# Gates by tanh, a last block in batch pairs, more turns on the matrix engine and a new order in a gated recurrence with a feed-forward

## The chip, the cores and the metric

One core of a Trainium2 chip runs the kernel. The metric is the time of one execution on the device in microseconds, the median over the runs shown.

## What is computed

An attention of the mLSTM kind over 4 batches, 8 heads, 768 steps and head size 40, and behind it a gated feed-forward of width 320 (the heads side by side). Cut to what matters:

```
m_new = max(f_t + m, i_t);  f' = exp(f_t + m - m_new);  i' = exp(i_t - m_new)
C = f' C + i' v_t k_t^T;    n = f' n + i' k_t
y_t = sigmoid(o_t) * (C q_t) / max(|n q_t|, 1)

x = y of all heads side by side                       # (4, 768, 320)
gate = sigmoid(causal convolution of x over 5 steps, one filter per column)
out = (gate * (x @ w_val)) @ w_out
```

The feed-forward's three weights come as float64, everything else as float32.

## The kernel before

The 768 steps are cut into six blocks j of 128 and each block into two halves of 64. A unit u = (j, b) is one block of one batch; a step g of 48 is one half of a unit. For each step, `args` computes the exponents of the decay by one matmul and `expo` their exponential; `scores` multiplies keys by queries; `probs` masks and scales on DVE; `keyw` weighs the keys on POOL; `heads` applies them to the values and, in the same run of matmuls, makes the next state, which `state_out` copies on ACT behind the values, where the next step reads it. So the steps of one batch form a chain.

Ahead of that, queries and keys are prepared per block, batch and side (x = 0 queries, x = 1 keys): `prep_max` finds the largest value on ACT, `prep_hi` and `prep_lo` split the scaled numbers in two-byte parts, stacked in one of three tiles `stk`, and the stack is turned, either by a DMA transpose from SP's queue (`prep_tr`, line 402) or on PE by eight transposes and a copy on ACT (`turn_pe`, line 410, and `turn_out`). The function `TURN` picks the way: before, all of block 0 and the queries of block 1 go over PE, 12 turns.

Behind the heads, `norm_abs`, `norm_rec`, `norm_o` and `gate_o` divide and apply the output gate, `x_tr` transposes the unit's result and `x_copy` puts it into `xc` (two chunks of 128 columns) and `x3` (64 columns; batches 0 and 1 in the lower partitions, 2 and 3 in the upper). From these, `feed(j)` makes the feed-forward of a block: `conv` (one instruction on ACT and four on DVE per chunk), `sigmoid`, `val` (x @ w_val on PE), `z_mul` on DVE, `outp` on PE, a copy and a store. In the last block it runs in two parts, batches 0 and 1, then 2 and 3.

The gates i and f are scanned in log form on DVE at the start, spread through DRAM and gathered as matmul operands; the weights are converted from float64 by integer steps on DVE, POOL and ACT.

The order of all 1141 operations is written out by hand: `PLAN` gives each operation of each kind its place in one sequence, and each engine and each DMA queue works through its share of it strictly in that order. `BANKS` gives each matmul group one of eight PSUM banks. DMAs are issued from SP's queue, apart from the spreading of the gates, which ACT issues.

Of the kernel before, what the change touches and what calls it, by code (L numbers as in the profile page):

```python
# [16 lines left out]
NTK, NSTK, NDM, NPT, NKW, NOB, OJ = 4, 3, 4, 3, 3, 3, 3  # L17
PLAN = {
# [31 lines left out]
    "args": (  # L50
        "223 220 236 237 274 281 266 285 311 322 334 351 354 369 387 397 414 488 474 472 581 550 582 585 638 640 "
        "666 675 688 738 712 741 763 816 772 814 835 893 873 910 916 974 901 976 1029 1025 1035 1055"
    ),
    "expo": (
        "229 247 244 240 277 288 272 293 316 327 340 361 358 378 392 403 417 502 515 491 591 578 596 614 641 647 "
        "670 679 695 744 716 749 767 821 777 818 838 897 877 915 926 980 907 982 1036 1027 1039 1059"
    ),
    "scores": (
        "241 226 246 258 284 289 291 307 324 332 359 356 396 384 401 419 485 495 501 531 584 587 594 634 642 677 "
        "681 686 708 760 753 758 807 817 812 831 880 909 878 914 972 992 945 994 1033 1046 1048 1062"  # L60
    ),
    "probs": (
        "245 254 249 264 295 298 303 310 337 341 363 373 400 440 413 426 490 506 520 535 597 592 601 637 649 685 "
        "690 693 715 769 756 764 813 830 822 837 884 911 890 920 981 997 962 1017 1040 1049 1054 1065"
    ),
    "keyw": (
        "242 257 253 261 282 294 309 314 331 339 345 371 383 424 411 428 492 513 524 538 598 593 602 622 650 655 "
        "674 691 704 751 734 752 783 825 790 833 846 905 892 921 952 956 1041 1042"
    ),
    "heads": (  # L70
        "250 267 260 275 300 317 326 338 344 362 375 391 406 451 422 439 526 537 543 557 615 628 621 645 668 696 "
        "702 728 732 775 765 782 828 840 845 869 904 918 896 938 988 1009 998 1030 1050 1064 1060 1066"
    ),
    "state": (
        "263 280 270 283 312 323 333 352 355 438 386 399 415 465 436 482 533 546 554 564 624 636 630 654 684 703 "
        "710 733 739 803 774 800 832 871 859 874 913 928 902 946 999 1004 1056 1063"
    ),
    "nabs": (
        "278 287 335 346 370 427 489 497 567 563 643 653 705 735 784 793 863 881 959 957 1023 1034 1067 1069"
    ),  # L80
    "nrec": "290 347 437 500 568 656 736 794 882 960 1037 1070",
    "rs": (
        "299 304 357 365 446 442 504 509 573 571 660 662 747 746 802 799 885 888 963 965 1044 1043 1073 1075"
    ),
    "x": (
        "308 360 367 377 460 448 512 514 579 575 663 671 773 748 847 849 891 917 977 979 1057 1045 1079 1080"
    ),
    "x_tr": (
        "313 372 388 382 468 463 522 534 595 589 755 683 810 836 875 912 968 970 983 985 1068 1058 1083 1086"
    ),  # L90
    "xc": (
        "348 380 394 389 484 470 528 539 605 600 761 687 815 841 887 919 971 975 989 991 1072 1061 1091 1095"
    ),
    "w_d": "71 64 61 23 67 97 234 243 302 423",
    "w_v": (
        "88 113 140 142 149 170 154 186 192 204 224 227 233 235 238 239 259 268 271 279 315 321 379 393 407 416 "
        "434 445 464 473 467 471 477 479 494 503"
    ),
# [6 lines left out]
    ),  # L105
    "conv0": "450 447 519 612 609 603 805 780 770 930 936 922 995 1001 1018 1074 1081 1076 1097 1109 1107",
    "conv": (
# [4 lines left out]
    ),  # L112
# [7 lines left out]
    ),  # L120
    "od": (
        "620 743 707 709 762 850 848 844 898 903 944 942 987 990 1015 1013 1052 1053 1088 1092 1132 1135 1138 "
        "1140"
    ),
}
BANKS = {
    "turn": "035214670217",
    "args": "456253054116722220154136320117150322715637044021",
    "scores": "432504700614456444555014006335324055110067647044",
    "ph": "623501366516421627255123",  # L130
    "pc": "44375644173345241133224470663034305631416020700",
    "x_tr": "766401332772034403237672",
    "conv": "724753757036037640552",
    "val": "270507314471263371406",
    "outp": "403206323674017663512173",
}
ENG = {}


def TURN(j, x, i):  # L140
    return 1 if j == 0 or (x == 0 and j == 1) else 0
# [3 lines left out]
def tile_mlstm_gated_ffn(  # L145
# [78 lines left out]
    tk_ = ring(NTK, [P, L + H * (P + L)], F16, "tk")  # L224
# [9 lines left out]
    rs_ = ring(2, [P, H, D], F32, "rs")  # L234
# [16 lines left out]
    def fill_v(kind, default, out, v):  # L251
        eng(kind, default).memset(out, v)

# [142 lines left out]
    def turned(j, x, i):  # L396
        if x == 0:
            return tq_[j % 2][:, i]
        return tk_[(j * B + i) % NTK][:, L:].rearrange("k (h n) -> k h n", h=H)[:, :, 0:P]
# [51 lines left out]

    def heads(g):
        u, p = divmod(g, 2)
        j, b = divmod(u, B)
        if p == 0:
            ph[u] = bank("ph", u, H, DT)
        more = g < NG - 2 * B or p == 0
# [417 lines left out]
```

## Time and profile before

| | us |
|---|---|
| median of 3 runs | 237.76 |
| lowest, highest | 235.78, 238.15 |
| span of the profiled execution | 234.1 |

| engine | busy us | share of the span |
|---|---|---|
| PE (matmuls) | 183.8 | 78% |
| DVE | 188.3 | 80% |
| ACT | 172.8 | 74% |
| POOL | 109.0 | 47% |

The span runs from the first to the last instruction of one profiled execution; the runs are timed without a profile and include what lies around it. PE is the matrix engine, PEld its weight loads, DVE the vector engine, ACT the scalar engine, POOL GpSimd, SP the queue that issues most DMAs. A float32 matmul appears as two records. Busy shares are means over stages with different limits.

### The profile page before, as it was taken

The page shows a single profiled execution, that of the slowest core. Times are in us where ns is not written, and L with a number is a line of the kernel's source. Part 1 is how long each engine was busy: PE and PEld are TensorE (multiplying, and loading weights), DVE is VectorE, ACT ScalarE, POOL GpSimd, SP SyncE. Part 2 cuts the span into 40 slices and gives each one's busy share as a digit, 9 for nine tenths or more (in the row PEclk, how much of TensorE's full clock was granted, in tenths as well). Part 3 has the DMA queues.
Part 4 walks back from the last instruction along what each step waited for, and adds up shares of the span by engine and source line. Part 5 has one row for each costly group of instructions (what it writes and reads, how often), then busy time and mean ns, then how long its engine had stood idle before and what let it go on. Part 6 is the DMA issues. An engine that isn't in the chain of part 4 may idle for free.

```text
span 234.1 us, 6369 instructions
## 1 busy us (share of the span) xinstructions
PE 183.8 (78%) x2432; PEld 135.4 (58%) x2432; DVE 188.3 (80%) x409; ACT 172.8 (74%) x357; POOL 109.0 (47%) x165
## 2 busy tenths in 40 slices
PE   0016501888997578699899999998999999999993
PEld 0016401666886545476768776875876776785441
DVE  7969988998798799999998869958798295539920
ACT  4584993999999996989969889598965846344431
POOL 7656404387789637835378375534632000420000
PEclk9999999999998577999999999999999999999999
DMA  6999997999999999999989999999167110001011
GB/s 112 174 174 178 195 162 100 148 181 182 140 156 176 204 174 209 152 181 147 201 190 196 164 183 175 160 213 184 62 79 159 59 56 0 30 31 59 0 55 59
DMA packets 146599, 31.96 MB, mean 137 GB/s; under 512 B 142408, under 2 KB 145864, under 8 KB 146568
## 3 DMA queue, kind: packets, MB, share of 16 engines
q1 hardware_dynamic: 144936, 31.25, 87.8%
q10 hardware_dynamic: 1632, 0.30, 0.7%
q8 instruction: 19, 0.31, 0.6%
q14 instruction: 12, 0.10, 0.1%
HBM read 17.87 MB, written 4.23 MB: 94 GB/s over the span
## 4 chain that ended last, share of the span: by engine, by line
PE 42%; ACT 18%; DVE 16%; SPq 8%; DMA 7%; issue 6%; ACTq 1%; POOL 0%; POOLq 0%; DVEq 0%
PE pb L463 12%; PE pb L610 9%; DVE pb L545 7%; PE pb L581 5%; SPq L336 4%; PE pb L612 3%; PE pb L421 3%; PE pb L434 3%; ACT junk L353 3%; DMA sg<-in_o_gate_dram 3%; DMA nat<-in_q_dram 3%; ACT sg L558 2%; ACT stk L381 2%; PE pb L503 2%; SPq L844 2%
## 5 line engine op out<-in xcount | busy, mean ns | idle before, releaser
L463 PE MATMUL pb<-vc,pt 128*64 128x41 f32 (+1 forms) x768 | 54.8, 235 | 6.3 <-ACT vc L249 4.0
L463 PEld LDWEIGHTS pb<-vc,pt 128*64 128x64 f32 (+1 forms) x768 | 50.0, 143 | 13.9 <-ACT vc L249 6.2
L446 POOL TENSOR_TENSOR kw<-kp,dm 128x320 f32<-128x320 f32 (+1 forms) x44 | 33.5, 771 | 38.4 <-ACT dm L424 26.7
L465 PE MATMUL pb<-vc,kw 128*40 128x41 f32 (+1 forms) x704 | 44.1, 218 | 0.4 <-ACT dm L424 0.2
L439 DVE SCALAR_TENSOR_TENSOR pt<-pb,cmp,dm 128x512 f32<-128x512 f32 x48 | 34.4, 737 | 11.0 <-PE pb L434 8.6
L465 PEld LDWEIGHTS pb<-vc,kw 128*40 128x40 f32 (+1 forms) x704 | 39.6, 119 | 0.8 <-issue 0.3
L410 PE MATMUL pb<-ident,stk 128*120 128x128 f16 x96 | 12.4, 318 | 33.0 <-DVE stk L387 33.0
L387 DVE SCALAR_TENSOR_TENSOR stk<-nat,scl,stk 128x320 f16<-128x320 f32 x48 | 32.9, 705 | 4.9 <-POOL stk L383 2.5
L383 POOL TENSOR_SCALAR stk<-nat,scl 128x640 f16<-128x640 f32 x24 | 21.5, 903 | 23.4 <-DMA vc<-in_v_dram 11.4
L410 PEld LDWEIGHTS <-stk 128*120 128x120 f16 x96 | 10.8, 219 | 34.2 <-DVE stk L387 34.2
L491 POOL TENSOR_TENSOR rs<-sg,den 128x320 f32<-128x320 f32 x24 | 18.0, 769 | 26.2 <-DVE den L487 25.4
L545 DVE SCALAR_TENSOR_TENSOR pb<-xc,cwt,pb 128x512 f32<-128x512 f32 (+1 forms) x42 | 27.4, 672 | 2.9 <-ACT pb L541 2.4
L610 PE MATMUL pb<-wall,zt 128*128 128x320 f32 x96 | 29.1, 442 | 0.4 <-DVE zt L602 0.4
L424 ACT ACTIVATE dm<-pb 128x512 f32<-128x512 f32 x48 | 27.3, 596 | 2.3 <-PE pb L421 1.7
L353 ACT ACTIVATE junk<-nat 128x320 bf16<-128x320 f32 x48 | 22.5, 469 | 6.6 <-DMA nat<-in_q_dram 5.8
L381 ACT ACTIVATE stk<-nat,scl 128x640 f16<-128x640 f32 x24 | 19.0, 819 | 9.6 <-DVE scl L359 4.8
L434 PEld LDWEIGHTS <-tk 120*128 120x128 f16 x384 | 15.8, 99 | 11.7 <-issue 9.1
L249 ACT COPY vc<-pb 40x328 f32<-40x328 f32 x44 | 18.8, 433 | 4.9 <-PE pb L465 3.1
L434 PE MATMUL pb<-tq,tk 120*128 120x64 f16 x384 | 18.4, 195 | 4.7 <-ACT vc L249 2.6
L610 PEld LDWEIGHTS pb<-wall,zt 128*128 128x128 f32 x96 | 17.3, 189 | 8.1 <-issue 1.3
L249 POOL COPY kp<-nat 64x640 f32<-64x640 f32 x24 | 18.6, 778 | 3.3 <-DMA nat<-in_k_dram 2.1
L249 ACT COPY ob<-pb 128x320 f32<-128x320 f32 x24 | 9.4, 428 | 14.4 <-PE pb L612 13.9
(108 smaller groups left out, 348.1 us busy)
## 6 DMA issues: line engine op xcount, KB each, us to landing
vc<-in_v_dram SPq DMA_DIRECT2D x12, 320.0 KB
sg<-in_o_gate_dram SPq DMA_DIRECT2D x6, 640.0 KB
out_dram<-ob SPq DMA_DIRECT2D x24, 160.0 KB
nat<-in_k_dram SPq DMA_DIRECT2D x10, 320.0 KB
nat<-in_q_dram SPq DMA_DIRECT2D x10, 320.0 KB
nat<-in_k_dram SPq DMA_DIRECT2D x4, 160.0 KB
nat<-in_q_dram SPq DMA_DIRECT2D x4, 160.0 KB
raw<-in_moe_w_val_dram SPq DMA_DIRECT2D x2, 320.0 KB
```

The source lines that it names most:

```text
L249: (e.copy if e is nc.scalar else e.tensor_copy)(out, in_)
L353: nc.scalar.activation(junk, part(j, x, i), AF.Abs, accum_out=amx[j % 2][:, x, i : i + 1])
L381: nc.scalar.activation(o, v, AF.Copy, scale=f)
L387: nc.vector.scalar_tensor_tensor(t[:, :, lo : lo + D], part(j, x, i), scl[j % 2][:, x, i : i + 1], t[:, :, 0:D], op0=ALU.mult, op1=ALU.sub ...
L424: nc.scalar.activation(dm_[g % NDM], psd[g], AF.Exp)
L434: nc.tensor.matmul(pss[g][:, h], tk[h], tq[:, h], start=True, stop=True)
L439: nc.vector.scalar_tensor_tensor(pt_[g % NPT], pss[g], cmp_[j % 2][:, p, b : b + 1], dm_[g % NDM], op0=ALU.mult, op1=ALU.mult)
L446: eng("keyw", "P").tensor_mul(kw_[g % NKW][0:n], kp[0:n, p, b * H : (b + 1) * H], dm_[g % NDM][0:n, :, L - 1 : L].to_broadcast([n, H, D]),)
L463: nc.tensor.matmul(ph[u][p * L : (p + 1) * L, h], pt_[g % NPT][0:n, h], mv, start=True, stop=True)
L465: nc.tensor.matmul(pc[g][n0 : n0 + D, h], kw_[g % NKW][0:n, h], mv, start=True, stop=True)
L545: nc.vector.scalar_tensor_tensor(of(gt, c, b0, b1) if t == 4 else o, x, w, o, op0=ALU.mult, op1=ALU.add)
L610: nc.tensor.matmul(t, zz[0][:, c, b], wo[:, c], start=(c == 0), stop=False)
```

## The change

Both gates are computed by tanh: sigmoid(a) = (1 + tanh(a/2)) / 2. The additions of 1 go into the products that follow (`gate_o`, `z_mul`, now of three operands), the factors into the function's scale (0.25 for the convolution, whose input is twice as large, 0.5 for the output gate) and into the scale of the last copy (0.25). The output gate is computed by an instruction of its own per block (`tanh_o`), the convolution's gate by another (`gate_x`). The division moves: DVE multiplies heads and output gate first (`gate_o`), and POOL multiplies by the reciprocal behind it (`norm_x`).

In the last block the batches are taken in the order 0, 2, 1, 3, and its feed-forward runs in the pairs (0, 2) and (1, 3), which lie in different partition halves of `x3`; the gate is applied per chunk.

Turns on PE take all 128 columns of the stack in place of 120, and there are 23 of them: all 8 of block 0, and in each later block the queries of batch 0 and the keys of batches 0 and 2. 25 DMA transposes remain of 36. `PLAN` and `BANKS` are written anew for all 1155 operations.

```diff
+TURNS = (((0, 1, 2, 3), (0, 1, 2, 3)),) + (((0,), (0, 2)),) * 5
 def TURN(j, x, i):
-    return 1 if j == 0 or (x == 0 and j == 1) else 0
+    return i in TURNS[j][x]
...
+    def jb(u):
+        j, b = divmod(u, B)
+        return j, (0, 2, 1, 3)[b] if j == NJ - 1 else b
+
+    def both(q):
+        return slice(q, B, B2)
...
-            nc.tensor.transpose(t[0:K3, h], stack(j, x, i)[:, h, 0:K3], ident16)
+            nc.tensor.transpose(t[:, h], stack(j, x, i)[:, h], ident16)
...
-    def norm_o(u):
-        j, b = divmod(u, B)
-        eng("rs", "P").tensor_mul(
-            rs_[u % 2], og[j % 2][:, b * H : (b + 1) * H], den[u // 2 % 3][:, u % 2, :, None].to_broadcast([P, H, D])
-        )
-
     def gate_o(u):
-        nc.vector.tensor_mul(x_[u % 2], ph[u][:, :, 0:D], rs_[u % 2])
+        j, b = jb(u)
+        o = og[j % 2][:, b * H : (b + 1) * H]
+        nc.vector.scalar_tensor_tensor(y_[u % 2], o, 1.0, ph[u][:, :, 0:D], op0=ALU.add, op1=ALU.mult)
+
+    def norm_x(u):
+        d = den[u // 2 % 3][:, u % 2, :, None].to_broadcast([P, H, D])
+        eng("x", "P").tensor_mul(x_[u % 2], y_[u % 2], d)
...
-    def sigmoid(j, b0, b1):
-        if b1 - b0 < B:
-            for g in (gt[0][:, :, b0:b1], of(gt, 2, b0, b1)):
-                nc.scalar.activation(g, g, AF.Sigmoid)
-            return
-        jo = j + OJ
-        g = sg[:, ng[0] : ng[1]]
-        if jo < NJ:
-            g = sg[:, 0 : ng[1]] if jo % 2 == 0 else sg[:, ng[0] :]
-        nc.scalar.activation(g, g, AF.Sigmoid)
-
-    def sig_o(j):
-        nc.scalar.activation(og[j % 2], og[j % 2], AF.Sigmoid)
+    def gate_x(j, c, qs):
+        g = sg[:, ng[0] : ng[1]] if c is None else of(gt, c, qs)
+        nc.scalar.activation(g, g, AF.Tanh, scale=0.25)
+
+    def tanh_o(j):
+        nc.scalar.activation(og[j % 2], og[j % 2], AF.Tanh, scale=0.5)
...
-            nc.vector.tensor_mul(of(zz, m, b0, b1), s, of(gt, m, b0, b1))
+        nc.vector.scalar_tensor_tensor(o, t, 1.0, s, op0=ALU.add, op1=ALU.mult)
...
-        copy("ob", "A", ob_[(j * B + b) % NOB], pot[j, b])
+        nc.scalar.activation(obs(j, b), pot[j, b], AF.Copy, scale=0.25)
...
     def feed(j):
-        n = B if j < NJ - 1 else B2
-        for b in range(0, B, n):
-            feed_part(j, b, b + n)
+        for qs in [(0, 1)] if j < NJ - 1 else [(0,), (1,)]:
+            feed_part(j, qs)
```

## Rows read from the trace of the kernel before

**Rows 1.** Stages: window, us, PE, PEld, DVE, ACT, POOL busy, clock, DMA share, GB/s.
```profile
0.00:44.10 44.10, 11.07 (x88) 9.86 (x89) 38.89 (x104) 29.72 (x57) 23.30 (x47) 1.00 1.05 153
44.10:75.00 30.90, 27.28 (x585) 21.74 (x584) 26.68 (x54) 29.77 (x69) 23.76 (x30) 1.00 1.25 173
75.00:95.00 20.00, 14.04 (x183) 10.49 (x182) 18.27 (x42) 17.89 (x42) 12.11 (x18) 0.66 1.17 189
95.00:120.00 25.00, 22.66 (x327) 16.78 (x327) 24.05 (x49) 21.56 (x49) 12.99 (x20) 1.00 1.36 173
120.00:208.00 88.00, 86.58 (x1173) 64.85 (x1171) 66.08 (x130) 63.85 (x121) 35.39 (x51) 1.00 0.73 122
208.00:234.10 26.10, 22.12 (x84) 11.66 (x81) 14.32 (x35) 10.01 (x23) 1.41 (x2) 1.00 0.11 39
```

**Rows 2.** ACT's table loads by line: count, busy us, mean ns, idle before.
```profile
L424 ACT ACT_TABLE_LOAD x7 | 9.0, 1283 | 0.1
...
L558 ACT ACT_TABLE_LOAD x5 | 6.4, 1283 | 2.1 <-DMA sg<-in_o_gate_dram 2.0
...
L561 ACT ACT_TABLE_LOAD x2 | 2.6, 1283 | 0.0
...
L552 ACT ACT_TABLE_LOAD x1 | 1.3, 1283 | 0.0
```

**Rows 3.** ACT in order of time, 45 to 106 us: start, us, instruction.
```profile
45.61 1.28 ACT L424 ACT_TABLE_LOAD   x1
...
74.37 0.60 ACT L424 ACTIVATE dm<-pb 128x512 f32<-128x512 f32 x1
74.99 1.28 ACT L561 ACT_TABLE_LOAD   x1
76.28 1.27 ACT L561 ACTIVATE sg<-sg 128x1280 f32<-128x1280 f32 x1
...
105.45 1.28 ACT L424 ACT_TABLE_LOAD   x1
```

**Rows 4.** The chain that ended last, in order of time: start, us, what.
```profile
64.98 0.47 PE pb L434 x16
...
126.94 3.46 PE pb L581 x16
...
145.78 6.83 DMA sg<-in_o_gate_dram
...
162.61 0.74 PE pb L612 x4
...
179.03 0.81 PE pb L503 x6
...
229.76 0.75 PE pb L612 x2
```

**Rows 5.** PE in order of time, 0 to 75 us.
```profile
19.06 3.82 PE L410 MATMUL pb<-ident,stk 128*120 128x128 f16 x32 [6.33 <-DVE stk L387]
...
51.39 0.39 PE L421 MATMUL pb<-ra,la 120*128 120x512 bf16 x1
```

**Rows 6.** Groups by line, shapes apart: count, busy us, mean ns, idle before.
```profile
L439 DVE SCALAR_TENSOR_TENSOR pt<-pb,cmp,dm 128x512 f32<-128x512 f32 x48 | 34.4, 737 | 11.0 <-PE pb L434 8.6 <-ACT ob L249 1.5 <-ACT dm L424 0.6
...
L496 DVE TENSOR_TENSOR x<-pb,rs 128x320 f32<-128x320 f32 x24 | 11.2, 482 | 2.2 <-POOL rs L491 2.0
...
L249 ACT COPY tq<-pb 120x1024 f16<-120x1024 f16 x8 | 7.9, 1008 | 0.0
L545 DVE SCALAR_TENSOR_TENSOR pb<-x,cwt,pb 128x256 f32<-128x256 f32 x15 | 7.3, 485 | 0.3
```

**Rows 7.** The same by line, PE alone, 0 to 50 us.
```profile
L421 PE MATMUL pb<-ra,la 120*128 120x512 bf16 x4 | 2.1, 634 | 0.0
```

**Rows 8.** All engines in order of time, 206 to 234 us.
```profile
212.15 1.03 PE L575 MATMUL pb<-xc,wall 128*128 128x256 f32 x4
...
221.32 0.70 PE L575 MATMUL pb<-x,wall 64*128 64x256 f32 x2
```

More of the change, by code (lines that the diff above doesn't have):

```diff
@@ L125 @@
 }
 BANKS = {
[L127 to L135, printed above, removed]
+    "turn": "01001243574114110600026",
+    "args": "541542634463677365600163040614473663377412732672",
@@ L136 @@
+    "scores": "621074744012433161453752573775344072230316103376",
+    "ph": "516101766035532654736275",
+    "pc": "60225522555744333344576622160034136655424040202",
+    "x_tr": "677274354451543624670730",
+    "conv": "143536435302360157635",
+    "val": "205024172516413702412",
+    "outp": "021741671547407530463214",
 }
 ENG = {}
+TURNS = (((0, 1, 2, 3), (0, 1, 2, 3)),) + (((0,), (0, 2)),) * 5
 def TURN(j, x, i):
-    return 1 if j == 0 or (x == 0 and j == 1) else 0
+    return i in TURNS[j][x]
@@ L427, in scores @@
         u, p = divmod(g, 2)
-        j, b = divmod(u, B)
+        j, b = jb(u)
         k0 = [p * P + h * (P + L) for h in range(H)]
-        tk = [tk_[u % NTK][0:K3, c : c + P] for c in k0]
+        tk = [tk_[b][0:K3, c : c + P] for c in k0]
         tq = tq_[j % 2][0:K3, b, :, p * L : (p + 1) * L]
@@ L544, in conv, with val @@
         else:
[L545 to L561 removed]
+            nc.vector.scalar_tensor_tensor(of(gt, c, qs) if t == 4 else o, x, w, o, op0=ALU.mult, op1=ALU.add)
+    def gate_x(j, c, qs):
[3 more added lines that the diff above has]
+        nc.scalar.activation(og[j % 2], og[j % 2], AF.Tanh, scale=0.5)
     vt, pot = {}, {}
[L565 removed]
+    def val(n, j, ms, qs):
         x, y = xc[j % 2], x3[j % 2]
[L567 to L576 removed]
+        nq = len(qs)
+        ts = [bank("val", n + i, 2 * nq if ms[0] < 2 else nq, P) for i in range(len(ms))]
+        vt[j, ms[0], qs[0]] = ts
+        bs = [slice(i * B2 + qs[0], i * B2 + qs[0] + nq) for i in range(2)]
+        yq = y[:, qs[0] : qs[0] + nq, 4:]
+        if len(ms) == 2:
             for m in range(2):
@@ L579, in val @@
                     for i, t in enumerate(ts):
-                        o = t[:, m * B2 : (m + 1) * B2]
-                        nc.tensor.matmul(
-                            o, wv[:, c, cs[m]], x[:, c, i * B2 : (i + 1) * B2, 4:], start=(m == 0 and c == 0), stop=False
-                        )
+                        w = wv[:, c, m * P : (m + 1) * P]
+                        o = t[:, m * nq : (m + 1) * nq]
+                        nc.tensor.matmul(o, w, x[:, c, bs[i], 4:], start=(m == 0 and c == 0), stop=False)
             for m in range(2):
@@ L586, in val @@
                     r = half(i * B2)
-                    o = t[:, m * B2 : (m + 1) * B2]
-                    nc.tensor.matmul(o, wv3[r, i, cs[m]], y[r, :, 4:], start=False, stop=(m == 1))
+                    o = t[:, m * nq : (m + 1) * nq]
+                    nc.tensor.matmul(o, wv3[r, i, m * P : (m + 1) * P], yq[r], start=False, stop=(m == 1))
         else:
@@ L591, in val, with z_mul, outp @@
                 for i in range(2):
-                    w, s = (wv[:, c], x[:, c, i * B2 : (i + 1) * B2, 4:]) if c < 2 else (wv3[:, i], y[:, :, 4:])
-                    nc.tensor.matmul(ts[0][i * L : i * L + L], w[:, cs[0]], s, start=(c == 0), stop=(c == 2))
-    def z_mul(j, m, i, b0, b1):
-        s = vt[j, m, b0][i]
-        if b1 - b0 == B and m == 0:
-            bs = slice(i * B2, (i + 1) * B2)
-            nc.vector.tensor_mul(zz[0][:, :, bs], s.rearrange("p (m b) t -> p m b t", m=2), gt[0][:, :, bs])
-        else:
-            s = s[half(b0)] if m == 2 and b1 - b0 < B else s
-            nc.vector.tensor_mul(of(zz, m, b0, b1), s, of(gt, m, b0, b1))
-    def outp(j, bs):
-        n = j * B + (2 * bs[0] if len(bs) > 1 else bs[0])
-        pf = [bank("outp", n + i, DM) for i in range(len(bs))]
+                    w, s = (wv[:, c], x[:, c, bs[i], 4:]) if c < 2 else (wv3[:, i], yq)
+                    nc.tensor.matmul(ts[0][i * L : i * L + L], w[:, 2 * P :], s, start=(c == 0), stop=(c == 2))
+    def z_mul(j, m, i, qs):
+        s = vt[j, m, qs[0]][i]
+        nq = len(qs)
+        if m == 0:
+            bs = slice(i * B2 + qs[0], i * B2 + qs[0] + nq)
+            o, t, s = zz[0][:, :, bs], gt[0][:, :, bs], s.rearrange("p (m b) t -> p m b t", m=2)
+        else:
+            bs = slice(qs[0], qs[0] + nq)
+            o, t = zz[1][:, bs], gt[1][:, bs]
+        nc.vector.scalar_tensor_tensor(o, t, 1.0, s, op0=ALU.add, op1=ALU.mult)
+    def outp(j, q):
+        bs = (q, q + B2)
+        pf = [bank("outp", j * B + 2 * q + i, DM) for i in range(2)]
         for t, b in zip(pf, bs):
@@ L611, in outp, with obs @@
         for t, b in zip(pf, bs):
-            nc.tensor.matmul(t, zz[1][half(b), b % B2], wo3[half(b), b // B2], start=False, stop=True)
+            nc.tensor.matmul(t, zz[1][half(b), q], wo3[half(b), b // B2], start=False, stop=True)
+    def obs(j, b):
+        return ob_[(j * B + b % B2 * 2 + b // B2) % NOB]
     def outp_st(j, b):
-        copy("ob", "A", ob_[(j * B + b) % NOB], pot[j, b])
+        nc.scalar.activation(obs(j, b), pot[j, b], AF.Copy, scale=0.25)
     def out_dma(j, b):
-        eng("od", "S").dma_start(out[b, j * P : (j + 1) * P, :], ob_[(j * B + b) % NOB])
+        eng("od", "S").dma_start(out[b, j * P : (j + 1) * P, :], obs(j, b))
     raw = ring(2, [P, DM, 2] if wide else [P, DM], I32 if wide else F32, "raw")
@@ L702, in tile_mlstm_gated_ffn @@
         op("c_p", fill, io_[:, 0:D], [[-1, D]], -r0)
-    for i in range(NTK):
+    for i in range(B):
         for x in range(2):
@@ L734, in prep, with feed_part @@
             op("tr", prep_tr, j, x, i)
-    def feed_part(j, b0, b1):
+    def feed_part(j, qs):
+        full = len(qs) == B2
         for c in range(3):
@@ L739, in feed_part @@
             for t in range(5):
-                op("conv" if t else "conv0", conv, n, j, c, t, b0, b1)
-        op("sig", sigmoid, j, b0, b1)
-        for ms in ((0, 1), (2,)) if b1 - b0 == B else ((0,), (1,), (2,)):
-            op("val", val, 3 * j + ms[0] + 3 * (b0 // B2), j, ms, b0, b1)
+                op("conv" if t else "conv0", conv, n, j, c, t, qs)
+            if not full:
+                op("sig", gate_x, j, c, qs)
+        if full:
+            op("sig", gate_x, j, None, qs)
+        for ms in ((0, 1), (2,)):
+            op("val", val, 3 * (j + (qs[0] if not full else 0)) + ms[0], j, ms, qs)
             for i in range(len(ms)):
-                op("z", z_mul, j, ms[0], i, b0, b1)
-        for bs in [(b, b + B2) for b in range(B2)] if b1 - b0 == B else [(b,) for b in range(b0, b1)]:
-            op("outp", outp, j, bs)
-            for b in bs:
+                op("z", z_mul, j, ms[0], i, qs)
+        for q in qs:
+            op("outp", outp, j, q)
+            for b in (q, q + B2):
                 op("ob", outp_st, j, b)
@@ L778, in tile_mlstm_gated_ffn @@
             op("cmp", prep_cmp, j, 0, B)
-        for i in range(B):
-            for p in range(2) if i % 2 == 0 else ():
-                op("kpe", load_k, j, p, i // 2)
+        for n in range(B):
+            i = jb(j * B + n)[1]
+            for p in range(2) if n % 2 == 0 else ():
+                op("kpe", load_k, j, p, n // 2)
             prep(j, 0, i)
@@ L786, in tile_mlstm_gated_ffn @@
             op("halo", halo, j, c)
-        for b in range(B):
+        for u in range(j * B, j * B + B):
             if j > 0:
-                prep(j, 1, b)
-            u = j * B + b
+                prep(j, 1, jb(u)[1])
             for g in (2 * u, 2 * u + 1):
@@ L806, in tile_mlstm_gated_ffn @@
             for n in (u - 1, u):
[L807 to L808 removed]
+                op("y", gate_o, n)
+                op("x", norm_x, n)
                 op("x_tr", x_tr, n)
@@ L831, in tile_mlstm_gated_ffn @@
             op("ld_o", load_o, j + 2)
-        if j + 2 < OJ:
-            op("sig_o", sig_o, j + 2)
-        if j >= OJ - 2:
-            feed(j - OJ + 2)
-    for j in range(NJ - OJ + 2, NJ):
+            op("sig_o", tanh_o, j + 2)
         feed(j)
```

135 lines of the change are left out of this document (56 added, 79 removed), and 75 rows, old and new, of the table PLAN.

## The prediction

> **What bounds the kernel now.** I read the page first (busy shares, the forty slices, the chain that ended last), then the stage table, then the chain in order of time, then the lines. The stage table [rows 1] is the frame, and its busy times are summed here. No matrix work of weight runs in the first 44.1 us: PE is busy 11.07 us there, DVE 38.89 of 44.10. From then on PE is busy 27.28 + 14.04 + 22.66 + 86.58 + 22.12 = 172.7 of the remaining 190.0 us, so 17.3 us of PE idle are left. About 3.6 us of it are the last copy and store after PE's last matmul; the other 13.7 us lie nearly all before 120 us: 3.6 in 44.1 to 75, 6.0 in 75 to 95, 2.3 in 95 to 120, only 1.4 in 120 to 208. In 75 to 95 the granted clock averages 0.66, that is part of it at 1.2 GHz; were all of PE's 14.04 busy us there stretched in that ratio, 14.04 x 0.34 = 4.8 us more are lost. So the kernel has a start (44 us), a stretch to 120 us in which others feed PE too slowly (ACT is busy 29.77 of 30.90 us in 44.1 to 75, DVE 24.05 of 25.00 in 95 to 120), and then PE itself. 13.7 + 4.8 = 18.5 us is what a better feed could win; beyond this only less PE work or an earlier start counts.
>
> **The tables on ACT.** The sigmoid and the exponential alternate, and each change costs a load: 7 + 5 + 2 + 1 = 15 loads, 19.2 us [rows 2]. With tanh for both gates they go if tanh and the exponential share a table; one first load stays. What a change costs is seen on one of them [rows 3]: the exponential ends at 74.97, the load starts at 74.99 and the gate's function at 76.28, so it is 1.28 us and 0.03 of seams. The Trainium skill, "ScalarE: Activation LUTs", section "What ACT_TABLE_LOAD costs", adds a drain of about 1380 ns to each load, 2.66 us in all; by that, an estimate from the page, 15 x 2.66 = 39.9 us would go. The trace shows no such drain, and the sum goes by 19.2.
>
> All but the first of L561's two stand behind 44.1 us, fourteen or 18.0 us; five of these lie before 120 us, from 45.61 to 105.45 [rows 3]. Against them stand the copies of the added turns: 23 turns in place of 12, each with a copy of 1.008 us [rows 6], 11.1 us more. Net ACT gains about 7 us after the start, and of that some 2.4 us before 120 us, where it matters (five loads less, 6.4 us, against about four copies more). So this is no gift of 19 us: the load of ACT per block hardly falls. The gates' own time stays, since one function over 2560 columns becomes two over 1280. One more thing goes with the split: before, the gate of the convolution was computed in one instruction with a later block's output gate, and waited for that gate's load, which is on the chain with 6.83 us [rows 4]. Now it waits for the convolution alone.
>
> **The turns on PE.** In the code 10 turns stand ahead of the first heads (12 before) and 13 behind it. At the start 32 transposes took 3.82 us [rows 5], 0.119 each, 0.95 a turn. That is an upper bound, since PE was slow there: the same 512-column matmul took 634 ns among the first four [rows 7] and 0.39 us at 51.39 [rows 5]; besides, 120 stationary columns become 128. The nearest row with 128 two-byte stationary columns is that of the scores, 16 matmuls of 64 columns in 0.47 us [rows 4], 0.029 each, 0.24 a turn: the lower bound. A turn streams twice as many columns, so 0.5 a turn: 13 x 0.5 = 6.5, less the one turn that ran after 44.1 before (0.95): +5.5 us of PE (bounds +2.2 and +11.4). Eleven DMA transposes and their places in SP's queue go in exchange; no long wait for them is on the chain, so I give nothing for them.
>
> **The last block.** The six single val groups ran from 212.15 to 222.02 [rows 8], 9.9 us. Now it is two pair groups of 36 records of 128 columns. By columns from 16 records of 256 columns in 3.46 us (216 ns [rows 4]), 72 x 0.108 = 7.8; with the 64-row and 64-column ones running side by side less, about 6; by the 128-column transposes (6 in 0.81, 0.135 each) 9.7. I take 6.9, -3.0 us (bounds -3.9 and 0). Of the output matmuls, the 64-row ones of one batch took 0.75 and those of a pair also 0.74 [rows 4], so four become two: -1.5 us. At the end two copies follow the last matmul where one did: bounded by 0 and by a turn's copy of 1024 columns (1.008 us [rows 6]); for 320 columns I take +0.4. The tail's convolutions on DVE get fewer rows of half-empty partitions: 8 instructions of 256 columns (485 ns [rows 6]) become 128 columns wide, at most half of it, -1 to -2 us; PE is as full there, and I count nothing.
>
> **The rest.** The gating product on DVE (482 ns) becomes one of three operands. Its price lies between 485 ns for 256 columns and 737 for 512 of that kind, 0.55 for 320 [rows 6]: 24 x 0.07 = +1.7 us on DVE, spread, hidden while PE ends last; in 95 to 120 us, where DVE is full, it would be 0.4. The POOL product keeps its size but now comes after DVE's and waits for the reciprocal; behind it in POOL's queue stand the key products. The chain from reciprocal to transpose loses DVE's 0.48, and the PSUM bank of the heads is free without waiting for the reciprocal. The z products and the scaled last copy change their kind, not their size.
>
> **The start.** Ahead of the first exponential ACT loses two table loads (2.57) and one output gate of 1.27 [rows 3], and gains about one small step: -3 us. The gate loads go first in SP's queue, and the later chunks' gate steps move ahead of the first chunk's last ones. Bounds: 0, and -5.2, all of DVE's idle time before 44.1 [rows 1].
>
> **Idle and slow time.** 18.5 us now. Convolutions and val of the first block move forward against the attention (val 0 from place 562 of 1141 to 407 of 1155), so that PE has something to do while the recurrence waits; seven more weight conversions leave the full DVE stretch for the start; ACT gains 2.4 us. I take 9 us of the 18.5 as won; the bounds are 0 and 14.5.
>
> **Sum.** -3 + 5.5 - 3.0 - 1.5 + 0.4 - 9 = -10.6 us on the span of 234.1: 223.5. The median of the runs, 237.76, stands 3.7 above the profiled span; with that, 227.2 us.
>
> **Rivals.** Dense: the start gains 5, the val groups 3.9, and only 4 us of idle are left: -5 + 5.5 - 3.9 - 1.5 + 0.4 - 14.5 = -19.0, 218.8 us. For it: 120 to 208 us shows that PE can be kept busy 86.58 of 88.00 us. Chance 0.2.
>
> Absorbed: the idle is the recurrence's own (state copy, matmul, copy), which nothing here shortens, and stays at 18.5: -1.6, 236.2 us. For it: ACT's load per block hardly changes. Chance 0.13.
>
> Clock: transposes take the place of nothing that keeps PE warm, and the stretch at the low clock doubles: +4.8 on the forecast, 232.0 us. For it: the first four 512-column matmuls, right behind turns, were slow [rows 7]; against it: the 13 turns stand among heads. [...] Chance 0.08.
>
> Slower, by the turns: each of the 13 stands in PE's strict order, so if its stack or its bank is late, all heads behind it wait. At s us each the forecast is used up at s = 10.6/13 = 0.8, and 1% slower at 1.0; at 1.5 it is 243.0, 246.7 us. Before, the turns' place was the start, where nothing stood behind them. Chance 0.06.
>
> Tables apart: tanh gets its own load. The new order changes 21 times between gates and exponential; 12 of them come by the 24th of 48 steps and count in full (15.4), 9 half (5.8): 244.7, 248.4 us. The Trainium skill, "ScalarE: Activation LUTs", section "Table sets: the hidden batching unit", lists tanh with the exponential's set and with the sigmoid's; which one is loaded no row here shows. Chance 0.03.
>
> **How the numbers follow.** The forecast has 0.5 with a range of its own from 222 to 232. A measurement of this kernel can tell about 1% from no change (235.4 and 240.1 us). Faster: 0.5 + 0.2 + 0.08 + 0.03 of absorbed = 0.81; same 0.10, the rest of it; slower 0.06 + 0.03 = 0.09. The range leaves out half of dense below and the slower cases above with a little of absorbed: 218 to 237.
>
> **What would show it.** One table load; 23 turns with weight loads well under 0.2 us; PE's first 512-column matmul near 41 us; the idle of PE between 44 and 120 us at half of 11.9; the last val groups in about 7 us; the last block's output matmuls in two groups of 12 records. A PE that waits before turns for DVE's stack, or a granted clock under 1 in a longer stretch, would prove me wrong; so would a first matmul still at 44.

## The result and the profile after

| | before | changed |
|---|---|---|
| median of the runs, us | 236.77 (4 runs) | 229.24 (4 runs) |
| lowest, highest | 235.15, 238.15 | 228.86, 229.85 |
| span of the profiled execution | 234.1 | 227.0 |
| ratio of the times, 95% interval | | 0.971 (0.965 to 0.976) |

The change makes the kernel 2.9% faster, 7.5 us by the medians and 7.1 by the spans. The forecast was 227.2 us, with 218 to 237 around it.

The stages between 44.1 and 120 us in the changed kernel, with the columns of [rows 1] (window, its length, busy us of PE, PEld, DVE, ACT and POOL with their instructions, clock, DMA share, GB/s):

```profile
44.10:75.00 30.90, 26.12 (x441) 21.22 (x442) 28.27 (x62) 25.57 (x64) 23.56 (x30) 0.94 1.18 172
75.00:95.00 20.00, 18.95 (x300) 14.03 (x298) 18.45 (x39) 17.61 (x35) 9.97 (x13) 1.00 1.18 143
95.00:120.00 25.00, 23.78 (x273) 16.66 (x273) 17.08 (x31) 22.12 (x56) 8.35 (x12) 1.00 1.26 188
```

Set them beside [rows 1]: 75 to 95 us has become another stretch. PE is busy 18.95 us there, not 14.04, and the clock is 1.00 instead of 0.66. DVE, 24.05 of 25 us busy in 95 to 120 before, is down to 17.08.

To see where the 7.1 us came from, cut both traces at the first heads, at 120 us and at the end of the last heads (208.12 us before, 203.10 after). First the kernel before, then the changed one:

```profile
0.00:48.97 48.97, 15.10 (x125) 12.40 (x125) 43.21 (x113) 34.56 (x66) 24.62 (x49) 1.00 1.06 156
48.97:120.00 71.03, 59.95 (x1056) 46.47 (x1056) 64.68 (x133) 64.38 (x150) 47.55 (x65) 0.90 1.27 177
120.00:208.12 88.12, 86.70 (x1174) 64.92 (x1173) 66.08 (x130) 63.85 (x121) 35.39 (x51) 1.00 0.72 122
208.12:234.10 25.98, 22.00 (x81) 11.59 (x81) 14.32 (x35) 10.01 (x23) 1.41 (x2) 1.00 0.11 39
```

```profile
0.00:49.20 49.20, 15.44 (x119) 10.72 (x120) 45.33 (x120) 31.86 (x66) 29.15 (x51) 1.00 1.04 166
49.20:120.00 70.80, 66.02 (x995) 50.20 (x994) 58.85 (x117) 62.39 (x146) 39.84 (x53) 0.98 1.21 168
120.00:203.10 83.10, 81.18 (x1317) 63.41 (x1316) 69.33 (x140) 59.88 (x121) 40.82 (x60) 1.00 0.57 92
203.10:227.00 23.90, 20.12 (x130) 13.82 (x129) 12.60 (x34) 9.19 (x26) 1.40 (x2) 1.00 0.15 56
```

PE's idle time is window minus busy time. It is 33.87 against 33.76 us up to the first heads, 11.08 against 4.78 from there to 120 us, 1.42 against 1.92 after that and 3.98 against 3.78 in the tail. So 6.3 us of idle went, all of it between the first heads and 120 us. PE's busy time fell by 1.0, from 183.75 to 182.76. The start gave nothing: the first heads run at 49.20 us, where they ran at 48.97.

What filled PE there is seen in its groups between the first heads and 120 us (records, busy us, mean ns, idle time just before them), heads and output matmuls, first of the kernel before, then of the changed one:

```profile
L463 PE MATMUL pb<-vc,pt 128*64 128x41 f32 (+1 forms) x384 | 29.2, 240 | 5.9 <-ACT vc L249 4.0 <-DVE pt L439 1.1 <-ACT dm L424 0.8
L610 PE MATMUL pb<-wall,zt 128*128 128x320 f32 x16 | 4.7, 439 | 0.0
```

```profile
L464 PE MATMUL pb<-vc,pt 128*64 128x41 f32 (+1 forms) x320 | 23.9, 240 | 0.8 <-ACT vc L243 0.7
L600 PE MATMUL pb<-wall,zt 128*128 128x320 f32 x32 | 9.5, 441 | 0.5 <-DVE pt L440 0.5
```

A step has 16 records of `heads`. So by 120 us the changed kernel has done 20 of the 48 steps where the old one had done 24, but twice the output matmuls: the feed-forward stands where PE had waited for the recurrence, and of the 6.3 us of idle 5.1 are the wait ahead of the heads, 5.9 before and 0.8 now.

### The profile page after: what moved, and what is told of

Read it like the earlier page. It is cut to its first block, busy times and chain, and to the rows that moved or that the text cites. A ratio compares the mean times of both kernels' runs of the same rounds, so it can differ in the third digit from the quotient of the medians.

```text
span 227.0 us, 6544 instructions
## 1 busy us (share of the span) xinstructions
PE 182.8 (80%) x2556; PEld 138.2 (61%) x2556; DVE 186.1 (82%) x409; ACT 163.3 (72%) x358; POOL 111.2 (49%) x165
## 4 chain that ended last, share of the span: by engine, by line
PE 45%; DVE 25%; ACT 10%; issue 6%; DMA 6%; SPq 5%; POOL 2%; ACTq 0%; DVEq 0%
PE pb L464 13%; PE pb L600 7%; PE pb L571 6%; DVE stk L388 5%; DVE pb L547 4%; DVE pt L440 4%; PE pb L422 3%; PE pb L581 3%; PE pb L435 3%; SPq L337 3%; PE pb L505 3%; DMA nat<-in_q_dram 2%; PE pb L602 2%; PE pb L466 2%; ACT junk L354 2%
## 5 line engine op out<-in xcount | busy, mean ns | idle before, releaser
L464 PEld LDWEIGHTS pb<-vc,pt 104*64 104x64 f32 (+1 forms) x768 | 48.8, 142 | 10.2 <-issue 4.9
L464 PE MATMUL pb<-vc,pt 104*64 104x41 f32 (+1 forms) x768 | 53.7, 235 | 1.5 <-ACT vc L243 0.7
L411 PE MATMUL pb<-ident,stk 128*128 128x128 f16 x184 | 18.1, 259 | 20.6 <-DVE stk L388 19.0
L388 DVE SCALAR_TENSOR_TENSOR stk<-nat,scl,stk 128x320 f16<-128x320 f32 x48 | 31.7, 681 | 1.2 <-ACT stk L382 0.5
L498 POOL TENSOR_TENSOR x<-y,den 128x320 f32<-128x320 f32 x24 | 18.0, 760 | 26.1 <-DVE den L489 22.8
L411 PEld LDWEIGHTS <-stk 128*128 128x128 f16 x184 | 14.0, 117 | 23.3 <-issue 13.5
L384 POOL TENSOR_SCALAR stk<-nat,scl 128x640 f16<-128x640 f32 x24 | 22.4, 941 | 8.6 <-PE pb L411 4.7
L571 PE MATMUL pb<-xc,wall 128*128 128x256 f32 (+1 forms) x112 | 24.2, 371 | 0.5 <-ACT x L243 0.5
L422 PE MATMUL pb<-ra,la 120*128 120x512 bf16 x48 | 18.8, 417 | 6.2 <-ACT tq L243 2.1
L571 PEld LDWEIGHTS pb<-xc,wall 128*128 128x128 f32 x112 | 19.6, 200 | 3.9 <-ACT x L243 0.9
```

Of the source, the lines that this page charges most:

```text
L388: nc.vector.scalar_tensor_tensor(t[:, :, lo : lo + D], part(j, x, i), scl[j % 2][:, x, i : i + 1], t[:, :, 0:D], op0=ALU.mult, op1=ALU.sub ...
L411: nc.tensor.transpose(t[:, h], stack(j, x, i)[:, h], ident16)
L464: nc.tensor.matmul(ph[u][p * L : (p + 1) * L, h], pt_[g % NPT][0:n, h], mv, start=True, stop=True)
L571: nc.tensor.matmul(o, w, x[:, c, bs[i], 4:], start=(m == 0 and c == 0), stop=False)
```

## The experiments

Each is timed against the kernel before on the same chip. Ratios are to that kernel, which took 236 to 237 us each time; the changed kernel stands at 0.971, and distances from it by the ratios are those of two kernels that were each timed against the kernel before. Three of them (e3, e9, e11) have a step on the wrong side of another's write to the buffer that it reads, so that it works on another block's data; their times do not answer the question that was asked.

### The tables: e1 and e2

```diff
- nc.scalar.activation(g, g, AF.Sigmoid)
+ nc.scalar.activation(g, g, AF.Tanh)          # e1, all three places of the kernel before
- nc.scalar.activation(g, g, AF.Tanh, scale=0.25)
+ nc.scalar.activation(g, g, AF.Sigmoid, scale=0.25)   # e2, both places of the changed kernel
```

> The kernel before with tanh written in place of the sigmoid at its three gate instructions, everything else as it was; the additions and factors that make a sigmoid of a tanh are left out, so the gates have other values. Fourteen of the fifteen table loads go, about 18 us of ACT at 1.283 each, and nothing else. If the loads feed PE's idle time (the forecast's view): the two ahead of the first heads give 2.6 us, the five between 44 and 120 us some 2 to 4 more, the rest nothing, 4 to 7 us below the kernel before (230 to 233 us against 236.8). If the place in the order decides what waits and the loads are hidden: 0 to 2 us below (235 to 237 us).

Measured: 234.77 us, ratio 0.994 (0.991 to 0.997), 1.4 us below the kernel before by the ratio. ACT's busy time fell from 172.8 to 153.4 us, and next to nothing followed. The second theory holds: in the old order the loads were hidden. The stage table of e1, its third and fourth rows:

```profile
75.00:95.00 20.00, 13.85 (x166) 9.84 (x165) 17.50 (x41) 14.54 (x39) 11.41 (x16) 0.58 1.25 193
95.00:120.00 25.00, 22.28 (x354) 17.28 (x353) 24.56 (x48) 20.40 (x48) 13.60 (x20) 0.99 1.27 173
```

ACT has 5.5 us free in 75 to 95 us where it had 2.1 [rows 1]. PE is as idle there as before, at as low a clock, and DVE is as full in 95 to 120. So it was not ACT's table loads that starved PE there.

> The changed kernel with the sigmoid's function in place of tanh at its two gate instructions (other gate values, same operations otherwise). The new order goes 21 times between a gate and the exponential, so about 22 loads come back, 21 x 1.283 = 27 us of ACT, with ACT busy 163 of 227 us before it. If ACT's instructions stand on the path: 10 to 20 us over the changed kernel (239 to 249 us). If ACT has room for them: up to 5 over (229 to 234 us).

Measured: 247.42 us, ratio 1.047 (1.042 to 1.052), 18.2 us above the changed kernel and 11.5 above the kernel before. The first theory holds. The loads of e2 (count, busy us, mean ns, idle before), as in [rows 2]:

```profile
L425 ACT ACT_TABLE_LOAD x10 | 12.8, 1283 | 0.2
...
L554 ACT ACT_TABLE_LOAD x6 | 7.7, 1283 | 0.1
L551 ACT ACT_TABLE_LOAD x5 | 6.4, 1283 | 0.1
...
L243 ACT ACT_TABLE_LOAD x1 | 1.3, 1283 | 0.7 <-PEq L851 0.7
```

Twenty-one more loads than the changed kernel's one are 26.9 us of ACT, and two thirds of that, 18.2 us, reach the end. The new order puts an exponential behind a gate and a gate behind an exponential as the recurrence wants them, and that is affordable only while both functions share a table. So tanh alone is worth 1.4 us, and the new order without it loses. ACT's timeline of e2 shows one pair of changes (start, duration, line, tiles):

```profile
84.91 0.42 ACT L243 COPY vc<-pb 40x328 f32<-40x328 f32 x1
85.34 1.28 ACT L425 ACT_TABLE_LOAD   x1
86.64 0.60 ACT L425 ACTIVATE dm<-pb 128x512 f32<-128x512 f32 x1
...
91.16 0.60 ACT L425 ACTIVATE dm<-pb 128x512 f32<-128x512 f32 x1
91.77 1.28 ACT L551 ACT_TABLE_LOAD   x1
93.06 1.27 ACT L551 ACTIVATE sg<-sg 128x1280 f32<-128x1280 f32 x1
```

A load starts within 0.02 us of the end before it, and the function 0.01 to 0.02 behind it. The drain of about 1380 ns that the Trainium skill, "ScalarE: Activation LUTs", section "What ACT_TABLE_LOAD costs", adds to each load does not show in these rows. With it, an estimate from the page, 21 loads would be 55.9 us of ACT; by the rows they are 26.9.

### The turns: e4, e5, and e3 and e9

```diff
 def TURN(j, x, i):
-    return i in TURNS[j][x]
+    return j == 0 or (j, x, i) == (1, 0, 0)      # e3, e5
-            nc.tensor.transpose(t[:, h], stack(j, x, i)[:, h], ident16)
+            nc.tensor.transpose(t[0:K3, h], stack(j, x, i)[:, h, 0:K3], ident16)   # e4
```

> The changed kernel with its 23 turns over 120 columns of the stack, as before, and not 128; the copies behind them are the same. If the width sets the price (0.95 us a turn as at the start of the kernel before, 0.5 with 128 columns): 13 turns behind the first heads lose 0.45 each, up to 6 us, 3 to 6 with cover taken off (232 to 235 us). If the 0.95 was a slow PE at the start and not the width: within 1 us of the changed kernel (228.5 to 230.5 us), and a turn in the middle of the kernel still takes about 0.5.

Measured: 229.25 us, ratio 0.971 (0.967 to 0.975), the changed kernel's time. The second theory holds. PE's timeline shows one turn of e4 and the same one of the changed kernel:

```profile
88.72 0.66 PE L411 MATMUL pb<-ident,stk 128*120 128x128 f16 x8
```

```profile
88.63 0.62 PE L411 MATMUL pb<-ident,stk 128*128 128x128 f16 x8
```

The eight overlap with their neighbours' ends; in the chain this turn counts 0.55 us in the changed kernel, others 0.45. The 0.95 us of [rows 5] was PE at the start, not the width: the changed kernel's turn at 44.75 us, with all 128 columns, takes 1.03.

> The changed kernel with 14 of its 23 turns given back to DMA transposes, issued from SP's queue right behind the step that finishes the stack; the 8 turns of block 0 and the first of block 1 stay. PE does about 14 x 0.5 = 7 us less, ACT 14 us less. If PE is the bound behind 50 us and the DMA path is free: 3 to 6 us below the changed kernel (223 to 226 us). If the turns on PE buy shorter waits than a transpose by DMA (the stack's three buffers come free later, the heads wait for keys or queries): 1 to 8 us above it (230 to 237 us).

> The changed kernel with 14 of its 23 turns given back to DMA transposes, each now placed behind both the finished stack and the last scores that read the keys or queries it replaces (in e3 some key transposes stood ahead of the scores of the block before, so that e3 prices that wait and not the turns). PE does 14 x 0.5 = 7 us less, ACT 14 us less. If PE is the bound and the DMA path is free: 3 to 6 us below the changed kernel (223 to 226 us). If the turns on PE buy a shorter way (0.5 us and a copy of 1.0, against transposes by DMA of 2.8 to 6.9 us on e3's chain): 1 to 8 us above it (230 to 237 us).

e3, with five of its key transposes ahead of scores that still read the old keys, took 244.17 us. e5, which keeps the order of writes and reads, took 241.47 us, ratio 1.019 (1.015 to 1.023): some 12 us above the changed kernel and 4.5 above the kernel before. It had 14 us less of ACT's copies to do (ACT busy 150.5 us instead of 163.3) and 7 less of PE's turns. So the second theory holds, by more than it gave. The chain of e5 between 84 and 108 us, its longest pieces (start, duration, what), and ACT's timeline there (idle time and its releaser in brackets):

```profile
86.61 4.67 DMA tq<-stk
...
92.05 4.20 DMA tq<-stk
...
97.90 6.93 DMA tk<-stk
```

```profile
92.18 0.83 ACT L382 ACTIVATE stk<-nat,scl 128x640 f16<-128x640 f32 x1 [1.89 <-DMA tk<-stk]
...
104.86 0.83 ACT L382 ACTIVATE stk<-nat,scl 128x640 f16<-128x640 f32 x1 [5.07 <-DMA tk<-stk]
```

Three transposes by DMA hold 15.8 of these 24 us, and it is the stack that waits for them: with three stack buffers ACT cannot write the next one before the transpose has read the last, and all that ACT has queued behind it waits too. A turn on PE reads the stack in half a microsecond. The 14 transposes stand in e5's order right behind the finished stack or the last scores that read what they replace; everything else keeps the places that were written for turns. So e5 prices turns against transposes in this order; an order written around these transposes was not tried. The stage table of e5, then of the changed kernel:

```profile
50.00:120.00 70.00, 56.41 (x865) 42.96 (x865) 56.34 (x114) 50.32 (x126) 36.90 (x49) 0.98 1.20 179
120.00:203.00 83.00, 75.96 (x1198) 57.76 (x1196) 59.77 (x125) 53.85 (x117) 42.74 (x63) 0.96 0.72 122
```

```profile
50.00:120.00 70.00, 65.58 (x991) 49.91 (x992) 58.08 (x116) 61.98 (x145) 39.04 (x52) 0.98 1.20 168
```

PE's idle time in 50 to 120 us is 13.6 us in e5 and 4.4 in the changed kernel: without the 14 turns there is more idle than the kernel before has (11.08 from its first heads to 120 us). Behind 120 us, up to 203, it is 7.0 against 1.9.

```diff
-    return 1 if j == 0 or (x == 0 and j == 1) else 0
+    return j == 0 or (j == 1 and (x == 0 or i in (0, 2))) or (j > 1 and i in ((0,), (0, 2))[x])   # e9
```

> The kernel before, its order and its sigmoid kept, with the same 14 turns that e5 gave back now put on PE in place of DMA transposes (26 turns; each stands about a third of the way from the place of the old transpose to the scores that need it, its copy on ACT five places behind). If a turn only adds work, as the forecast's sum has it: 14 x 0.5 = 7 us of PE and 14 us of ACT in the sigmoid's order, 3 to 9 us above the kernel before (240 to 246 us). If a turn on PE is worth its price because the DMA transpose is late by several us in 75 to 120 us, as e5 says of the new order: 2 to 6 us below (231 to 235 us). If its worth comes only with an order written for it: within 2 us of it.

e9 took 253.67 us, ratio 1.075 (1.071 to 1.078). Seven of its 14 turns stood behind the step that writes their stack anew, and PE, strictly in order, waited for it. What these turns would do in the old order by themselves stays open.

### The pairs of the last block: e8

```diff
 # outp, last block: the 64-row matmul straight behind the two 128-row ones of its batch
+            if j == NJ - 1:
+                nc.tensor.matmul(t, zz[1][half(b), q], wo3[half(b), b // B2], start=False, stop=True)
 # val, last block: one half of the array after the other, not alternately (so too for the 64-row ones)
-            for c in range(3):
-                for i in range(2):
+            for k in range(6):
+                for c, i in [(k // 2, k % 2) if nq == B2 else (k % 3, k // 3)]:
```

> The changed kernel with the last block's matmuls of 64 rows or 64 columns no longer side by side: the val and output groups do the same matmuls, but those of one half of the array first and then those of the other. By the changed kernel's own rows a pair then loses 0.34 in the 64-row val matmuls, 0.68 in the 64-column ones and 0.75 in the output's, 1.8 us, two pairs 3.5 us. If the pairing is what the tail gains: 2.8 to 3.8 us above the changed kernel (232 to 233 us). If the tail waits for something else than PE: 0 to 1 us above it (229 to 230 us).

Measured: 232.05 us, ratio 0.980 (0.976 to 0.983), 2.1 us above the changed kernel by the ratios and 2.5 by the spans. The chain of the tail, first of the changed kernel, then of e8 (start, duration, what):

```profile
206.48 0.81 PE pb L581 x12
...
210.98 1.98 PE pb L571 x16
212.96 0.65 PE pb L576 x8
213.61 0.81 PE pb L581 x12
214.41 1.98 PE pb L571 x16
216.40 0.65 PE pb L576 x8
217.04 2.35 PE pb L600 x8
219.39 0.74 PE pb L602 x4
```

```profile
213.78 0.65 PE pb L576 x8
214.44 1.07 PE pb L581 x12
...
218.14 1.27 PE pb L600 x4
219.42 0.73 PE pb L602 x2
220.15 1.27 PE pb L600 x4
221.42 0.73 PE pb L602 x2
```

The output groups cost what was expected: four times 2.00 against twice 3.09, 1.8 us. The 64-column val matmuls (L581) cost 0.26 a pair, not 0.68, and the 64-row ones of val (L576) nothing: 0.65 either way, and whether they overlap in either order is not shown. 1.8 + 2 x 0.26 = 2.4 us of the 2.5 between the spans. So the pairing is worth this in the tail, less than the 2.8 to 3.8 that the first theory gave.

### The start and DVE: e6, e10, e12, and e11 and e7

The changed kernel's POOL and DVE ahead of the first heads (timeline, idle time in brackets):

```profile
47.16 1.10 POOL L630 TENSOR_TENSOR cv<-cv,cv 128x320 f32<-128x320 f32 x1 [4.56 <-DVE cv L629]
48.22 2.42 POOL L447 TENSOR_TENSOR kw<-kp,dm 104x320 f32<-104x320 f32 x3
```

```profile
46.59 0.49 DVE L629 SCALAR_TENSOR_TENSOR cv<-raw,cv 128x320 int32<-128x320 int32 x1
47.00 0.55 DVE L388 SCALAR_TENSOR_TENSOR stk<-nat,scl,stk 128x320 f16<-128x320 f32 x1
47.46 1.41 DVE L440 SCALAR_TENSOR_TENSOR pt<-pb,cmp,dm 128x512 f32<-128x512 f32 x2
```

The exponentials of the first steps were done at 45.3 us, but a weight conversion stood ahead of their key products on POOL and of their masks on DVE. So two experiments moved conversions behind the first heads, only by their places in `PLAN`:

```diff
-    "w_v": "... 241 244 247 250 265 ...",  "w_p": "... 253 ..."
+    "w_v": "... 272.1 272.3 272.5 272.7 283.2 ...",  "w_p": "... 280.5 ..."   # e10, its main moves; e6: those of 199 to 406
```

> The changed kernel with the weight conversion's steps that stand at places 207 to 406 of the order (DVE, POOL, ACT and their loads) moved to 285 to 405, behind the first heads; nothing else. Theory (the three microseconds forecast for the start were lost to conversions ahead of the first heads: POOL's product for them waited 4.56 us for DVE's conversion, the first keys' product stood behind it): the first heads start 2 to 4 us earlier, at 45 to 47 against 49.2 us, and the time falls by 1 to 4 us (225 to 228 us). Rival (the conversions only push DVE's work into 50 to 75 us, which is as full): heads start earlier, but the stretch behind loses it again, 0 to 2 us above the changed kernel (229 to 231 us).

> The changed kernel with the fourth weight conversion alone (five DVE steps at places 241 to 265, POOL's product at 253) moved behind the masks of the first three steps, nothing of the loads and of the conversions ahead of it; in e6 the first heads came 3.8 us earlier, but the loads of the last third of w_val with them later, and val 0 ran 4.1 us later. Theory (start decides once the weights come no later): heads start at 46.5 to 48 against 49.2 us, val 0 where it was, 1 to 2.5 us below the changed kernel (226.7 to 228.2 us). Rival (50 to 75 us is held by DVE's and ACT's load, not by when it starts): within 0.7 us of it (228.5 to 230 us) or above.

Measured: e6 234.34 us, ratio 0.990 (0.986 to 0.993), 4.5 us above the changed kernel by the ratios. e10 232.11 us, ratio 0.979 (0.974 to 0.984), 2.1 above. In e6 the heads start at 45.40 us and yet val 0, the first feed-forward work, comes later. PE's timeline at the start of val 0 in the changed kernel, in e6 and in e10:

```profile
71.42 0.80 PE L571 MATMUL pb<-xc,wall 128*128 128x256 f32 x1 [0.53 <-ACT x L243]
```

```profile
75.56 2.93 PE L568 MATMUL pb<-xc,wall 128*128 128x256 f32 x6 [0.32 <-ACT x L240]
```

```profile
73.58 1.65 PE L568 MATMUL pb<-xc,wall 128*128 128x256 f32 x3 [0.53 <-ACT x L240]
```

4.1 and 2.2 us late, about what the times lost, though e10's runs lie apart (229.09 to 235.01 us) and its interval touches the changed kernel's. The last wait ahead of val 0 is in all three for a copy of the heads' result (`x`, on ACT), not for the weights. The rivals hold, in e6 with more than twice the loss that they allowed: what goes from the start comes back in 50 to 75 us, where e6's PE is busy 17.36 us instead of 22.84, at a clock of 0.77 instead of 0.93. e10's heads came no more than 0.1 us earlier (49.13): with POOL's step gone, the matmuls ahead of them waited 1.50 us for DVE's masks.

```diff
-        op("w_a", lambda: nc.scalar.activation(xf, hi.bitcast(F32), AF.Abs))
-        op("w_v", lambda: V.scalar_tensor_tensor(dst, xf, F64_MIN, dst, op0=ALU.is_ge, op1=ALU.mult))   # e12
```

> The changed kernel without the last step of the weight conversions, the guard that sets weights below the smallest float32 to zero (left out: six products on DVE, 3.5 us, two of them with 1.5 us ahead of the first heads, and six absolute values on ACT, 2.7 us); the places of everything else are kept. Theory (DVE, busy 87.1 of the first 95 us, bounds that stretch, which is why e6 and e10 won nothing by reordering it): val 0 starts 2 to 4 us earlier than 71.4 and the time falls by 1.5 to 3.5 us (225.7 to 227.7 us). Rival (that stretch waits for the recurrence or for loads, and reordering failed for its places alone): within 0.8 us of the changed kernel (228.4 to 230 us).

Measured: 226.97 us, ratio 0.962 (0.958 to 0.965), 2.1 us below the changed kernel and the lowest of all. Reordering this work lost time; taking some of it away, 3.5 us from DVE and 2.7 from ACT, won 2.1. Which of the two engines gave it e12 does not tell apart. The profiled execution of e12 was the longest of its seven (229.94 us), so only its first half is read: the first heads start at 48.04 and val 0 at 70.31, both 1.1 us earlier. That is about half of the least that the theory gave for val 0, though the time is within its 1.5 to 3.5. Half of the gain is there by 70 us then; the rest is not located. As it stands this is no better kernel for all inputs, since the guard is part of the conversion.

```diff
-    "w_v": "... 238 ...",  "lo": "... 252 ..."
+    "w_v": "... 269.2 ...",  "lo": "... 269.4 ..."   # e11, besides e10's places
```

> As e10, and besides DVE's last step of the third conversion (place 238) and one stack of block 1 (252) moved behind the masks of the first steps, another 1 us of DVE ahead of the first heads. Theory: heads start 0.7 to 1 us before e10's and the time is 0.5 to 1 us below e10's. Rival (the stack or the conversions are wanted earlier than that): no gain on e10, or a loss.

e11 took 240.50 us, ratio 1.019 (1.015 to 1.023). The stack it moved stood behind a load (place 259) that overwrites that stack's queries, so it says nothing of the start.

```diff
-    "max": "... 618 622 638 640 ..."
+    "max": "... 668.41 672.41 688.41 690.41 ..."   # e7
```

> The changed kernel with the largest values of the last block's queries (four instructions on ACT at places 618 to 640) 50 places later; ACT waited 1.52 us there for a load of 5.45 us, ahead of an exponential. If this wait holds the recurrence (DVE idle 1.67 us in 110 to 120 us): 1 to 2 us below the changed kernel (227 to 228.3 us). If PE's order has work in that stretch anyway: within 0.6 us of it (228.6 to 229.8 us).

Measured: 230.37 us, ratio 0.973 (0.970 to 0.976): the rival, 0.5 us above the changed kernel by the ratios and not below it. PE is busy 10.00 of 10 us in 110 to 120 where it was 9.53, and the end did not move.

## Why the prediction came out right, and where its steps did not

**The sum.** It gave 223.5 us for the span, 3.5 less than 227.0. Most of that is the start, below. The offset of 3.7 from span to median was too large: the changed kernel's profiled execution took 228.86 us with a span of 227.0, 1.9 apart. The 3.7 held the spread of the old kernel's executions besides, 235.78 to 238.15. The two misses partly cancel, which leaves 227.2 against 229.24: that the forecast came so near is in part luck.

**The start, -3 forecast, 0 measured: the step that failed.** PE's first 512-column matmul did come at 40.10 us, as the prediction wanted to see, 4 us earlier than before. But this sign stands too early in the chain. Between it and the first heads stand masks on DVE and key products on POOL, and the conversions that the prediction itself counted as "seven more" for the start stood ahead of both. e6 shows that 3.8 us are to be had at the heads and that they are then lost before val 0. The start was no term of its own.

**The tables, a gain of 2.57 us at the start and some 2.4 us before 120.** The row was right: each load 1.28 us and no drain. The step from ACT's time to the end was too generous for the old order, where all loads were worth 1.4 us (e1), and too small for the new one, where they would cost 18.2 (e2). The rival of tables apart had 21 changes and 248.4 us; e2, with exactly these changes, took 247.42. Tanh and the exponential do share a load: the changed kernel has one. That agrees with the Trainium skill, "ScalarE: Activation LUTs", section "Table sets: the hidden batching unit", which has tanh in the exponential's set.

**The turns, +5.5.** The price was right: 0.45 to 0.55 us each in the chain, and PE's busy time on turns rose from 12.4 to 18.1 us, 5.7 where +5.5 was forecast. The other side of the exchange was set at nothing, "no long wait for them is on the chain", read from the old order. In the new one 14 transposes by DMA cost some 12 us more than 14 turns (e5). So in this order the turns are no cost that the rest must win back; they are a condition of the gain, and the sign of the exchange as a whole was wrong.

**The last block, -3.0, -1.5 and +0.4.** Val: 6.06 us from 210.98 to 217.04 and 0.81 at 206.48, where one pair's 64-column matmuls stand, so 6.9 us against 9.9 [rows 8], -3.0 as forecast. Outputs: four groups of 2.00 us became two of 3.09, -1.8; e8 confirms it. The end: 3.73 us behind PE's last matmul against 3.6, +0.1. Together -4.7 instead of -4.1.

**Idle and slow time, -9.** Idle went down by 6.1 us over the whole span. The slow clock, estimated at 4.8 us before, is left in 70 to 75 us only, where PE is busy 4.32 us at 0.66, 1.5 by the same reckoning. 6.1 + 3.3 = 9.4, so the size was right, though between 44.1 and 120 us 7.0 of the 11.9 us of idle are left and not half. Its reasons held in part. The prediction named the earlier val 0, the moved conversions and 2.4 us of ACT. The first is in the rows: the first 128-column val matmuls of block 0 run at 71.42 us where they ran at 100.6, and the wait ahead of the heads is gone. But it is not enough: e2 and e5 keep the places of val 0 and of the conversions and lose the gain, one without tanh and one without the turns. In the new order neither can be missed. What val 0's place is worth by itself was not tried. The prediction did read DVE's full stretch in 95 to 120 us, and DVE's time between first heads and 120 us fell from 64.68 to 58.85 us, but it gave this no weight of its own. Most of this is moved, not saved: up to 120 us DVE masks 22 steps instead of 25, and in the whole kernel it is busy 186.1 us instead of 188.3. e1 says that ACT's loads were not what starved PE in the old order, and e12 that the work of DVE and ACT in the first part still counts.

**What is over.** The sum with measured terms: 0 for the start, +5.7 for the turns on PE, -4.8 for the tail's matmuls, -9.4 for idle (the end in it) and clock make -8.5; the spans differ by 7.1. The rest, about 1.4 us of PE's work, I cannot place; since groups on PE overlap at their ends, this sum is not exact.

**The rivals.** Dense wanted 5 us at the start and 14.5 of idle and slow time; 0 and 9.4 came. Absorbed would have left 11 us of idle before 120; 4.8 are left, and what went is the recurrence's own wait. Clock: no second slow stretch came; the later turns stand among heads. That the first four 512-column matmuls were slow is no sign of the low clock in the rows: the clock reads 1.00 in both stages around them [rows 1]. Slower by turns: turns wait only ahead of the first heads, 20.6 us in all (33.0 before), not one behind them; the later ones are in the chain with their 0.45 to 0.55 us.

## What to carry to other kernels

Cost both sides of an exchange in the order that will run it: a wait that is absent from the old chain can be the new one's bound, as the transposes by DMA were. Parts that win little alone may still be needed for each other, so a sum over parts can be right in size with wrong signs inside. Other work put where the matrix engine waits for a recurrence takes the wait away without making the recurrence any faster. And an earlier start of the matrix work was no gain by itself here: e6, with the heads 3.8 us earlier and the same work, lost 4.5 us, while e12, with less work, won 2.1.

## What the runs showed of the hardware

- Turns of 128 and of 120 two-byte columns cost the same time in the kernel (229.24 and 229.25 us), though the weight loads take 117 ns with 128 columns and 169 with 120 on average.
- A DMA transpose of one stack took 2.8 to 6.9 us in e5's chain, at a DMA share of 0.72 to 1.20 in its stages.
- In the first 45 us the granted clock reads 1.00 in the rows, 2.4 GHz, while the same 512-column matmul takes 0.59 us at 40.10 that takes 0.38 at 70.51, and a turn 1.03 instead of 0.62. The column reads 1.00 in the first 5 us too, where PE runs nothing. What slows PE at the start is not shown by the granted clock.
